# A fused pooled-attention and four-expert kernel: the first group's head is rebuilt around an early F32 load of its queries

## The chip, the cores and the metric

The kernel runs on one core of one Trainium2 chip. The metric is device time in microseconds (us) of one launch. The kernel before was run three times: 553.23, 553.50 and 553.97, median 553.5 us.

## The reference, cut to what matters

There are 8 batches with 8 heads, 576 tokens and 64 values per head. Keys and values are averaged over runs of 8 tokens, so each head has 72 pooled rows. The attention output becomes 4608 rows of 512, and four expert networks are summed over it with weights from `domain_probs`.

```python
k_p = k.reshape(B, H, 72, 8, 64).mean(axis=3)      # v_p likewise
scores = (q @ k_p.T) / 8
attn = exp(scores - max(scores))
attn = attn / (sum(attn) + 1e-9)
x = (attn @ v_p)  ->  rows of tokens, 512 columns (8 heads x 64)
p = domain_probs / (domain_probs.sum(-1) + 1e-9)
out = sum over e of p[:, e] * (relu(x @ w1[e]) @ w2[e])   # w1 512x1024, w2 1024x512
```

## The kernel before, in words

**Tiles and groups.** Tokens go in tiles of 128 (36 tiles, index `t`), four tiles to a group of 512 (9 groups). A tile of attention is: `turn_q` (four transposes on TensorE into PSUM, copy on ScalarE), `scores` (four products of 144 columns, two heads each), `less_max` (maximum and subtraction on VectorE), `expo` (ScalarE), `normalise` (sums, reciprocal and scaling on VectorE), `attn_T` (five transposes, copy), `context` (products with the values, copy into `xT`, the transposed input of the experts). From tile 8 on (`by_dma`) the transposes are DMA transposes on SP's queue, and the division is done on the context's rows instead.

**Keys and values.** A batch's 576 pooled rows lie on partitions in five blocks (the last has 64 rows, `TAIL`), with 8 x 64 values to a row. `fold` adds halves three times over on VectorE. `prep_k` multiplies the folded keys by `mask_k`, which puts each head's rows into its half of 128 columns, and `prep_kT` turns the result. `prep_v2` multiplies the folded values by `mask_v` into the block matrix `vbd`. Both masks are made on VectorE from `own`, which GpSimd makes with two selections.

**Experts.** `up` is one block of 128 hidden columns for a whole group (four products of 512 columns), `up_tile` is all 1024 hidden columns for one tile (32 products of 128 columns, L445), `down` (L462) is eight products of 512 columns for one tile, and `collect` adds the weighted result into `acc`.

**Order.** The order of every queue is the order in which the code is written; nothing is rescheduled. After the head, a loop of 36 steps (9 groups x 4 experts) with 12 slots each runs `up` of the next step and `down` of this one, and a plan puts the attention of later groups into its slots (`plan_tile`, `plan_batch`).

**The head** is all before that loop: the first batch's keys and values, group 0's four tiles, and expert 0's first tiles. Tile 0 must pass through the whole attention chain before the first `up_tile` can start. `idle_products(n)` runs `n` products of zeros (128x512) on TensorE; nothing reads their result. `split_q(c)` copies tile `c`'s rows of `qg`, the queries of group 0 as loaded, into `qrow[c]`.

**Loads.** All large loads are issued on GpSimd's queue (POOL), which casts F32 to BF16: keys of batch 0 in three pieces, `qg`, values, then weights, later keys, values and queries. A load waits for the one issued eight before it, so POOL's issues also tell when earlier loads landed. SP's queue loads `domain_probs` (`dp0`, `dpr`) at the start, and later does the DMA transposes and the output.

Of the kernel before, what the change touches and what calls it, by code (L numbers as in the profile page):

```python
# [10 lines left out]
ALU = mybir.AluOpType  # L11
AX = mybir.AxisListType
# [5 lines left out]
def kernel(  # L18
# [101 lines left out]
    def load_w2(e):  # L120
        nc.gpsimd.dma_start(
            out=w2_sb[e][:], in_=moe_w2[e].rearrange("(fb p) d -> p fb d", p=P)
        )

    dp0 = const.tile([P, TPG, E], F32, name="dp0")
    nc.sync.dma_start(
        out=dp0[:], in_=moe_domain_probs[0:G].rearrange("(p c) e -> p c e", c=TPG)
# [7 lines left out]
    still = const.tile([P, G], BF16, name="still")  # L137
    nc.vector.memset(still[:], 0.0)
    load_rows(kraw[0], k[0], ((0, 2), (2, 4)))
    qg = raw.tile([P, H, TPG, D], BF16, name="qg")  # L140
    nc.gpsimd.dma_start(
        out=qg[:], in_=q[0][:, 0:G, :].rearrange("h (p c) d -> p h c d", c=TPG)
    )

    own = const.tile([P, NPAIR, 2, 2], BF16, name="own")
    nc.gpsimd.memset(own[:], 1.0)
    for sign, base in ((1, 0), (-1, SP - 1)):
# [2 lines left out]
            base=base, channel_multiplier=sign,  # L150
            pattern=[[sign * (P - PW), NPAIR], [sign * P, 2], [-sign * SP, 2]],
        )
    ident = const.tile([P, P], BF16, name="ident")
    make_identity(nc, ident[:])
    load_v(0)
    load_w1(0)
    load_w2(0)
    load_w1(1)
    for c in range(TPG):
        qrow[c] = qpool.tile([P, H, D], BF16, name="qrow")  # L160
    ident32 = const.tile([NL, NL], F32, name="ident32")
    make_identity(nc, ident32[:])
    load_w2(1)
    load_w1(2)
    load_k(1)
    load_q(TPG)
    load_v(1)
    load_q(TPG + 1)
    load_q(TPG + 2)
    load_w2(2)  # L170
    load_w1(3)
    load_q(TPG + 3)
    load_w2(3)

    p_sb = const.tile([P, E, NT], F32, name="p_sb")
    ds0 = const.tile([P, TPG], F32, name="ds0")
    nc.vector.reduce_sum(out=ds0[:], in_=dp0[:], axis=AX.X)
    nc.vector.tensor_scalar_add(out=ds0[:], in0=ds0[:], scalar1=1e-9)
    nc.vector.reciprocal(out=ds0[:], in_=ds0[:])
    nc.vector.tensor_tensor(  # L180
        out=p_sb[:, :, 0:TPG].rearrange("p e c -> p c e"), in0=dp0[:],
        in1=ds0[:].unsqueeze(2).to_broadcast([P, TPG, E]), op=ALU.mult,
    )

    for t in (*kraw, *vraw):
        nc.vector.memset(t[TAIL:P, NB - 1, :], 0.0)
    for t in attn:
        nc.vector.memset(t[:, ROWS:NB * P], 0.0)

    mask_v = const.tile([P, NPAIR, 2, 2, D], BF16, name="mask_v")  # L190
    mask_k = const.tile([P, NB, 2, D], BF16, name="mask_k")
    nc.vector.tensor_copy(
        out=mask_v[:].rearrange("p a z y d -> p (a z y) d"),
        in_=own[:].rearrange("p a z y -> p (a z y)").unsqueeze(2).to_broadcast(
            [P, NPAIR * 4, D]
        ),
    )
    nc.vector.tensor_copy(out=mask_k[:, 0], in_=mask_v[:, 0, 0])
    nc.vector.tensor_add(
        out=mask_k[:, 1:NPAIR], in0=mask_v[:, 1:NPAIR, 0], in1=mask_v[:, 0:NPAIR - 1, 1]  # L200
    )
    nc.vector.tensor_copy(out=mask_k[:, NPAIR], in_=mask_v[:, NPAIR - 1, 1])
# [81 lines left out]
    def by_dma(t):  # L284
        return t >= 2 * TPG

    def turn_q(t):
        qT[t] = soft.tile([P, NPAIR, P], BF16, name="qT")
        if by_dma(t - 1):
            nc.sync.dma_start_transpose(  # L290
                out=qT[t][:], in_=qrow[t][:].rearrange("p h d -> p (h d)")
            )
            return
        ps = ps_t.tile([P, NPAIR, P], BF16, tag="t", name="qT_ps")
        for pair in range(NPAIR):
# [4 lines left out]
        nc.scalar.copy(out=qT[t][:], in_=ps[:])  # L300

    def scores(t):
# [7 lines left out]
                )  # L310
        scs[t] = sc

    def less_max(t):
        sc = scs.pop(t)
        view = sc[:, :, 0:2 * PW].rearrange("p g (h j) -> p g h j", j=SP)
        mx = soft.tile([P, 2, 4], F32, name="mx")
        nc.vector.reduce_max(out=mx[:], in_=view, axis=AX.X)  # L317
        d_sb = soft.tile([P, 2, 4, SP], F32, name="d_sb")
        nc.vector.tensor_tensor(  # L319
            out=d_sb[:], in0=view,  # L320
            in1=mx[:].unsqueeze(3).to_broadcast([P, 2, 4, SP]), op=ALU.subtract,
        )
        st[t] = d_sb

    def expo(t):
        if by_dma(t):
            nc.scalar.activation(  # L329
                out=attn[t % 2][:, 0:ROWS].rearrange("p (h j) -> p h j", j=SP),  # L330
                in_=st[t][:].rearrange("p g h j -> p (g h) j"),
                func=ACT.Exp, scale=EXP_SCALE,
            )
# [31 lines left out]
    def attn_T(t, copy=nc.scalar.copy):  # L365
# [6 lines left out]
            nc.tensor.transpose(ps[:, i, :], attn[t % 2][:, i * P:(i + 1) * P], ident[:])  # L372
        copy(out=attnT[t][:], in_=ps[:])  # L373

    def context_rows(t):
        ps = ps_t.tile([P, DM], F32, tag="t", name="x_ps")  # L380
        for b, _, n, at in segments(t * P, P):
            flat = vbd[b][:].rearrange("p a z y d -> p (a z y d)")
            for i in range(NB):
                c0, c1 = max(0, 4 * i - 1), min(4 * NPAIR, 4 * i + 2)
                h0 = max(0, 2 * i - 1)
# [12 lines left out]
        return x_sb  # L398
# [103 lines left out]

    def plan_tile(t, slot, turn=0):
        exp, norm, move, sum_v = (3, 4, 3, 8) if by_dma(t) else (4, 5, 8, 10)
        if t + TPG < NT and not by_dma(t):
            at(slot, load_q, t + TPG)
        at(slot + turn, turn_q, t)
        at(slot + 2, scores, t)
        at(slot + 2, less_max, t)
        at(slot + exp, expo, t)  # L510
        at(slot + move, attn_T, t)
        at(slot + norm, sums if by_dma(t) else normalise, t)
        at(slot + sum_v, context, t)
        if by_dma(t):
            at(slot + sum_v, gate, t)
            if t + TPG < NT:
                at(slot + sum_v, load_q, t + TPG)

    at(SLOTS - 4, domain_probs)
    at(SLOTS - 2, prep_k, 1)  # L520
    at(SLOTS, prep_kT, 1)
    at(SLOTS, prep_v, 1)
    at(SLOTS, load_k, 3)
    at(SLOTS, load_v, 3)
    for i, slot in enumerate((0, 4, 8, 12)):
        plan_tile(TPG + i, SLOTS + slot, -1 if i else 0)
    done_batches, waiting = 2, []
    for g in range(2, NG):
        for i in range(TPG):
            t = g * TPG + i  # L530
# [11 lines left out]


    def split_q(c):
        nc.vector.tensor_copy(out=qrow[c][:], in_=qg[:, :, c, :])  # L545
# [7 lines left out]
    prep_k(0, ((0, 2), (2, NB)))  # L553
    prep_kT(0, nc.scalar.copy)
    idle_products(4)
    split_q(0)
    turn_q(0)
    split_q(1)
    idle_products(1)
    scores(0)  # L560
    turn_q(1)
    less_max(0)
    expo(0)
    split_q(2)
    idle_products(3)
    fold(vraw[0], 0, NB, 4)
    scores(1)
    turn_q(2)
    idle_products(5)
    normalise(0)  # L570
    prep_v2(0)
    attn_T(0)
    idle_products(2)
    context(0)
    less_max(1)
    expo(1)
    up_tile(0, 0)
    scores(2)
    split_q(3)
    normalise(1)  # L580
    less_max(2)
    for t in range(1, TPG):
        if t == 1:
            turn_q(3)
        attn_T(t)
        if t + 1 < TPG:
            expo(t + 1)
        down(0, t - 1, 0, FB // 2)
        context(t)
        if t == 1:  # L590
            scores(3)
        down(0, t - 1, FB // 2, FB)
        up_tile(0, t)
        if t + 1 < TPG:
            normalise(t + 1)
        if t == 1:
# [48 lines left out]
```

## Time and profile before

| what | value |
|---|---|
| median of three runs | 553.5 us |
| profiled execution: time / span from first to last instruction | 555.25 us / 553.2 us |
| TensorE busy (matmul) | 533.0 us, 96% of the span |
| VectorE, ScalarE busy | 266.9 us, 212.0 us |
| mean granted clock of TensorE | 0.995 |
| read from memory | 45.16 MB |

The profile is of one execution. Rows of its timeline give the start, the duration, the engine (PE is TensorE's products, PEld its weight loads, DVE is VectorE, ACT is ScalarE, POOL is GpSimd, SPq is SP's queue), the line of the kernel, the operation, and what ended the idle time before it. A row with `x4` is a merged group of four instructions. The table of stages gives busy time of each engine in a stretch of time, the granted clock (1.00 is full), and what the DMA queues moved.

### The profile page before, as it was taken

The numbers are of one execution on the slowest core, as the hardware profiler recorded it, in microseconds if no ns is written. First come the engines' busy times: TensorE is split into PE (matmuls) and PEld (weight loads), VectorE is DVE, ScalarE is ACT, GpSimd is POOL, SyncE is SP. The second block draws the span as 40 slices with busy tenths as digits, with TensorE's granted clock in tenths as the row PEclk, the third lists the DMA queues.
The fourth block names the chain that finished last, engine by engine and source line by source line (L and its number), as shares of the span: only waits on it lengthen the run. The fifth ranks groups of instructions, "written<-read, shape, count | busy, mean of one in ns | idle before, by whom it ended". The sixth has DMA issues, their size and how long they took to land.

```text
span 553.2 us, 7201 instructions
## 1 busy us (share of the span) xinstructions
PE 533.0 (96%) x2837; PEld 260.0 (47%) x2892; DVE 266.9 (48%) x458; ACT 212.0 (38%) x352; POOL 71.9 (13%) x121
## 2 busy tenths in 40 slices
PE   2799999999999999999999999999999999999996
PEld 1574554444444444444444444444444444444443
DVE  4875657444744445544564444744474444422222
ACT  1455653333333333333333333333333333333330
POOL 7224311210111100121011100110010000000000
PEclk9899999999999999999999999999999999999999
DMA  9999995455345544366535553334333321111002
GB/s 137 207 206 197 203 123 109 68 80 80 75 86 79 79 78 80 53 84 87 113 44 78 78 116 41 52 42 97 61 53 41 87 52 32 21 39 38 1 0 76
DMA packets 110688, 45.30 MB, mean 82 GB/s; under 512 B 87584, under 2 KB 106016, under 8 KB 110656
## 3 DMA queue, kind: packets, MB, share of 16 engines
q0 software_dynamic: 52512, 22.55, 33.1%
q1 hardware_dynamic: 58144, 22.30, 16.8%
q8 instruction: 22, 0.36, 0.3%
q14 instruction: 10, 0.08, 0.0%
HBM read 45.16 MB, written 9.44 MB: 99 GB/s over the span
## 4 chain that ended last, share of the span: by engine, by line
PE 94%; DMA 2%; DVE 1%; issue 1%; ACT 1%; POOL 0%; ACTq 0%; POOLq 0%
PE o_ps L462 44%; PE h_ps L429 43%; PE x_ps L386 2%; PE sc L306 2%; PE h_ps L445 2%; DMA qg<-in_q_dram 2%; PE x_ps L412 1%; PE qT_ps L296 0%; ACT attnT L373 0%; POOL kraw L79 0%; ACT qT L300 0%; DVE vraw L225 0%; PE at_ps L372 0%; DVE qrow L545 0%; DVE vbd L270 0%
## 5 line engine op out<-in xcount | busy, mean ns | idle before, releaser
L433 ACT ACTIVATE h_sb<-h_ps 128x512 bf16<-128x512 f32 x280 | 167.2, 597 | 296.4 <-PE h_ps L429 289.8
L429 PE MATMUL h_ps<-xT,w 128*128 128x512 bf16 x1088 | 271.8, 379 | 1.5
L462 PE MATMUL o_ps<-w,h_sb 128*128 128x512 bf16 x1129 | 269.9, 379 | 1.4
L462 PEld LDWEIGHTS <-h_sb 128*128 128x128 bf16 x1152 | 112.3, 98 | 133.6
L477 DVE SCALAR_TENSOR_TENSOR acc<-o_ps,p_sb,acc 128x512 f32<-128x512 f32 x108 | 81.0, 750 | 180.1 <-PE o_ps L462 177.4
L429 PEld LDWEIGHTS <-w 128*128 128x128 bf16 x1120 | 105.9, 98 | 116.9
L473 DVE TENSOR_SCALAR acc<-o_ps,p_sb 128x512 f32<-128x512 f32 x36 | 27.0, 750 | 59.7 <-PE o_ps L462 59.7
L501 POOL COPY gated<-x_sb 1x1 bf16<-1x1 bf16 x28 | 7.8, 280 | 362.5 <-DVE x_sb L392 362.5
L317 DVE TENSOR_REDUCE mx<-sc 128x8 f32<-128x576 f32 x36 | 27.2, 756 | 13.4 <-PE sc L306 13.4
L107 POOL DMA_DIRECT2D qrow<-in_q_dram x36 | 30.5, 848 | 20.0 <-DMA w<-in_moe_w_dram 9.9
L319 DVE TENSOR_TENSOR d_sb<-sc,mx 128x576 f32<-128x576 f32 x36 | 27.3, 758 | 1.2
L392 DVE SCALAR_TENSOR_TENSOR x_sb<-x_ps,rs 128x512 bf16<-128x512 f32 x28 | 19.4, 692 | 12.1 <-PE x_ps L386 11.7
L350 DVE TENSOR_REDUCE es<-attn 128x8 f32<-128x576 bf16 x28 | 20.8, 743 | 0.0
L329 ACT ACTIVATE attn<-d_sb 128x576 bf16<-128x576 f32 x28 | 19.1, 682 | 3.2
L306 PE MATMUL sc<-kT,qT 128*128 128x144 bf16 (+1 forms) x160 | 15.5, 231 | 0.4 <-ACT qT L300 0.3
L306 PEld LDWEIGHTS <-qT 128*128 128x128 bf16 (+1 forms) x160 | 11.4, 102 | 9.6 <-ACT qT L300 1.7
L386 PEld LDWEIGHTS <-attnT 128*128 128x128 bf16 (+1 forms) x155 | 11.7, 100 | 7.2 <-issue 1.3
L386 PE MATMUL x_ps<-vbd,attnT 128*128 128x192 bf16 (+5 forms) x155 | 14.2, 231 | 0.0
L225 DVE TENSOR_TENSOR kraw<-kraw 128x1280 bf16<-128x1280 bf16 (+5 forms) x18 | 10.6, 589 | 2.3 <-DMA kraw<-in_k_dram 2.0
L225 DVE TENSOR_TENSOR vraw<-vraw 128x1280 bf16<-128x1280 bf16 (+1 forms) x16 | 10.5, 653 | 0.2
L255 PE MATMUL kT_ps<-ident,kpad 128*128 128x128 bf16 x10 | 1.2, 264 | 9.4 <-DVE kpad L240 9.4
L445 PE MATMUL h_ps<-xT,w 128*128 128x128 bf16 x128 | 9.3, 239 | 0.7 <-ACT xT L418 0.7
(61 smaller groups left out, 152.7 us busy)
## 6 DMA issues: line engine op xcount, KB each, us to landing
out_dram<-acc SPq DMA_DIRECT2D x36, 256.0 KB, 2.0
vraw<-in_v_dram POOLq DMA_DIRECT2D x8, 512.0 KB, 8.2
w<-in_moe_w_dram POOLq DMA_DIRECT2D x8, 512.0 KB, 15.7
w<-in_moe_w_dram POOLq DMA_DIRECT2D x4, 1024.0 KB, 16.9
kraw<-in_k_dram POOLq DMA_DIRECT2D x7, 512.0 KB, 7.2
qrow<-in_q_dram POOLq DMA_DIRECT2D x28, 128.0 KB, 3.9
kraw<-in_k_dram POOLq DMA_DIRECT2D x2, 256.0 KB, 4.7
kraw<-in_k_dram POOLq DMA_DIRECT2D x8, 64.0 KB, 6.8
```

The lines of the kernel that those rows point to most:

```text
L107: nc.gpsimd.dma_start(out=qrow[t][at:at + n], in_=q[b][:, tok:tok + n, :].rearrange("h p d -> p h d"),)
L225: nc.vector.tensor_add(out=rows[:, i0:i1, 0:w], in0=rows[:, i0:i1, 0:w], in1=rows[:, i0:i1, w:2 * w],)
L306: nc.tensor.matmul(sc[at:at + n, pair // 2, (pair % 2) * PW:(pair % 2 + 1) * PW], lhsT=qT[t][:, pair, at:at + n], rhs=kT[b][:].rearrange(" ...
L317: nc.vector.reduce_max(out=mx[:], in_=view, axis=AX.X)
L319: nc.vector.tensor_tensor(out=d_sb[:], in0=view, in1=mx[:].unsqueeze(3).to_broadcast([P, 2, 4, SP]), op=ALU.subtract,)
L350: nc.vector.reduce_sum(out=es[:], in_=e, axis=AX.X)
L386: nc.tensor.matmul(ps[at:at + n, h0 * D:(h0 + c1 - c0) * D], lhsT=attnT[t][:, i, at:at + n], rhs=flat[:, c0 * D:c1 * D], start=(i == 0), s ...
L429: nc.tensor.matmul(ps[:], lhsT=w1_sb[e][:, kc, fb * P:(fb + 1) * P], rhs=xT[g][:, kc, :], start=(kc == 0), stop=(kc == KC - 1),)
L433: nc.scalar.activation(out=hs[s][:, fb, :], in_=ps[:], func=ACT.Relu)
L462: nc.tensor.matmul(ps[:], lhsT=hs[s][:, fb, i * P:(i + 1) * P], rhs=w2_sb[e][:, fb, :], start=(fb == 0), stop=(fb == FB - 1),)
L473: nc.vector.tensor_scalar_mul(out=accs[t][:], in0=ps[:], scalar1=p_sb[:, e, t:t + 1])
L477: nc.vector.scalar_tensor_tensor(out=accs[t][:], in0=ps[:], scalar=p_sb[:, e, t:t + 1], in1=accs[t][:], op0=ALU.mult, op1=ALU.add,)
```

## The change

The head is written anew; the loop of steps stays, but for the slots of a few loads.

- **Queries.** `qg` becomes F32 and is loaded by SP as the first transfer of its queue; `split_q` moves from VectorE to ScalarE. Turned queries get a pool of four buffers.
- **Keys of batch 0.** They are folded in the three pieces in which they land, the last fold writes both halves of `kpad0` by a broadcast, without a mask. After the turn, two copies on VectorE take each head's rows out of PSUM into a zeroed `kT[0]`.
- **Tile 0.** The exponentials go undivided into `attn[0]`. Their sums come from TensorE (`sums0`, products with `own`), and the division is done on the context's rows (`context_rows`), which are then turned by four transposes (`turn_x0`).
- **Values of batch 0.** Eight accumulating products with the identity sum them in PSUM (`sum_values0`), and two VectorE instructions spread them with the mask (`spread_values0`).
- **Order.** More idle products stand between the steps; the masks and `dp0`'s normalisation come later; `down` of tile 0 comes after `up_tile` of tile 1; `prep_v(1)` is planned four slots later; POOL issues values before the identity and `own`, and the second batch's keys and expert 2's first weights ahead of expert 1's second weights. Later query loads are issued three tiles ahead, and batch 3's keys and values come later.

```diff
+    qg = raw.tile([P, H, TPG, D], F32, name="qg")
+    nc.sync.dma_start(
+        out=qg[:], in_=q[0][:, 0:G, :].rearrange("h (p c) d -> p h c d", c=TPG)
+    )
     dp0 = const.tile([P, TPG, E], F32, name="dp0")
...
     load_rows(kraw[0], k[0], ((0, 2), (2, 4)))
-    qg = raw.tile([P, H, TPG, D], BF16, name="qg")
-    nc.gpsimd.dma_start(
-        out=qg[:], in_=q[0][:, 0:G, :].rearrange("h (p c) d -> p h c d", c=TPG)
-    )
+    load_v(0)
+    ident = const.tile([P, P], BF16, name="ident")
+    make_identity(nc, ident[:])
...
     load_w1(0)
     load_w2(0)
     load_w1(1)
...
+    load_k(1)
...
+    load_w1(2)
+    load_q(TPG)
     load_w2(1)
-    load_w1(2)
-    load_k(1)
-    load_q(TPG)
+    load_q(TPG + 1)
     load_v(1)
...
+    def in_rows(t):
+        return t == 0 or by_dma(t)
+
     def turn_q(t):
-        qT[t] = soft.tile([P, NPAIR, P], BF16, name="qT")
+        qT[t] = qtp.tile([P, NPAIR, P], BF16, name="qT")
...
     def expo(t):
-        if by_dma(t):
+        if in_rows(t):
...
-        if t + TPG < NT and not by_dma(t):
-            at(slot, load_q, t + TPG)
...
-            if t + TPG < NT:
-                at(slot + sum_v, load_q, t + TPG)
+            if t + 3 < NT:
+                at(slot + sum_v, load_q, t + 3)
...
-    at(SLOTS, prep_v, 1)
-    at(SLOTS, load_k, 3)
-    at(SLOTS, load_v, 3)
+    at(SLOTS + 4, prep_v, 1)
...
-    done_batches, waiting = 2, []
+    done_batches, waiting = 2, [(load_k, 3), (load_v, 3)]
...
     def split_q(c):
-        nc.vector.tensor_copy(out=qrow[c][:], in_=qg[:, :, c, :])
+        nc.scalar.copy(out=qrow[c][:], in_=qg[:, :, c, :])
...
+    def fold_keys0(p1, i0, i1):
+        rows = kraw[0][0:p1, i0:i1]
+        for n in (4, 2):
+            w = n * D
+            nc.vector.tensor_add(
+                out=rows[:, :, 0:w], in0=rows[:, :, 0:w], in1=rows[:, :, w:2 * w]
+            )
+        twice = [p1, i1 - i0, 2, D]
+        nc.vector.tensor_tensor(
+            out=kpad0[0:p1, i0:i1], in0=rows[:, :, 0:D].unsqueeze(2).to_broadcast(twice),
+            in1=rows[:, :, D:2 * D].unsqueeze(2).to_broadcast(twice), op=ALU.add,
+        )
...
+    def sum_values0():
+        ps = ps_h.tile([P, NB, D], F32, tag="h", name="v_ps")
+        for r in range(POOL):
+            nc.tensor.matmul(
+                ps[:], lhsT=ident[:], rhs=vraw[0][:, :, r * D:(r + 1) * D],
+                start=(r == 0), stop=(r == POOL - 1),
+            )
+        return ps
...
+    idle_products(14)
+    split_q(0)
+    split_q(1)
+    turn_q(0)
+    turn_q(1)
+    for part in ((P, 0, 2), (P, 2, 4), (TAIL, 4, 5)):
+        fold_keys0(*part)
+        turn_keys0(*part)
+        idle_products(2)
+    take_keys0()
+    make_mask_v()
+    scores(0)
+    split_q(2)
+    turn_q(2)
+    less_max(0)
+    split_q(3)
+    expo(0)
+    idle_products(2)
+    spread_values0(sum_values0())
+    attn_T(0)
+    scores(1)
+    maxima(1)
+    idle_products(2)
+    sums0()
+    turn_q(3)
+    idle_products(1)
+    xT[0] = grp.tile([P, KC, G], BF16, name="xT")
+    x0 = context_rows(0)
     idle_products(4)
...
+    turn_x0(x0)
+    less(1)
+    expo(1)
     idle_products(2)
...
     up_tile(0, 0)
     scores(2)
-    split_q(3)
     normalise(1)
+    idle_products(4)
     less_max(2)
+    domain_probs0()
     for t in range(1, TPG):
-        if t == 1:
-            turn_q(3)
         attn_T(t)
         if t + 1 < TPG:
             expo(t + 1)
-        down(0, t - 1, 0, FB // 2)
+        if t == 1:
+            idle_products(3)
+        else:
+            down(0, t - 1, 0, FB // 2)
         context(t)
         if t == 1:
             scores(3)
-        down(0, t - 1, FB // 2, FB)
-        up_tile(0, t)
+            up_tile(0, t)
+            down(0, t - 1)
+        else:
+            down(0, t - 1, FB // 2, FB)
+            up_tile(0, t)
...
+        if t == TPG - 1:
+            make_mask_k()
         collect(0, t - 1)
+    load_q(2 * TPG)
     load_k(2)
+    load_q(2 * TPG + 1)
     load_v(2)
+    load_q(2 * TPG + 2)
```

More of the change, by code (lines that the diff above doesn't have):

```diff
@@ L57 @@
     qpool = ctx.enter_context(tc.tile_pool(name="qpool", bufs=8))
+    qtp = ctx.enter_context(tc.tile_pool(name="qtp", bufs=TPG))
     soft = ctx.enter_context(tc.tile_pool(name="soft", bufs=2))
@@ L152 @@
         )
-    ident = const.tile([P, P], BF16, name="ident")
-    make_identity(nc, ident[:])
-    load_v(0)
     load_w1(0)
@@ L160 @@
         qrow[c] = qpool.tile([P, H, D], BF16, name="qrow")
+    load_k(1)
     ident32 = const.tile([NL, NL], F32, name="ident32")
     make_identity(nc, ident32[:])
+    load_w1(2)
+    load_q(TPG)
     load_w2(1)
-    load_w1(2)
-    load_k(1)
-    load_q(TPG)
+    load_q(TPG + 1)
     load_v(1)
-    load_q(TPG + 1)
     load_q(TPG + 2)
-    load_w2(2)
     load_w1(3)
     load_q(TPG + 3)
+    load_w2(2)
     load_w2(3)
[L175 to L186, printed above, removed]
+    nc.vector.memset(vraw[0][TAIL:P, NB - 1, :], 0.0)
     for t in attn:
@@ L191, with make_mask_v, make_mask_k, domain_probs0 @@
     mask_k = const.tile([P, NB, 2, D], BF16, name="mask_k")
[L192 to L202, printed above, removed]
+    def make_mask_v():
+        nc.vector.tensor_copy(
+            out=mask_v[:].rearrange("p a z y d -> p (a z y) d"),
+            in_=own[:].rearrange("p a z y -> p (a z y)").unsqueeze(2).to_broadcast(
+                [P, NPAIR * 4, D]
+            ),
+        )
+    def make_mask_k():
+        for t in (*kraw, vraw[1]):
+            nc.vector.memset(t[TAIL:P, NB - 1, :], 0.0)
+        nc.vector.tensor_copy(out=mask_k[:, 0], in_=mask_v[:, 0, 0])
+        nc.vector.tensor_add(
+            out=mask_k[:, 1:NPAIR], in0=mask_v[:, 1:NPAIR, 0], in1=mask_v[:, 0:NPAIR - 1, 1]
+        )
+        nc.vector.tensor_copy(out=mask_k[:, NPAIR], in_=mask_v[:, NPAIR - 1, 1])
+    p_sb = const.tile([P, E, NT], F32, name="p_sb")
+    def domain_probs0():
+        ds0 = const.tile([P, TPG], F32, name="ds0")
+        nc.vector.reduce_sum(out=ds0[:], in_=dp0[:], axis=AX.X)
+        nc.vector.tensor_scalar_add(out=ds0[:], in0=ds0[:], scalar1=1e-9)
+        nc.vector.reciprocal(out=ds0[:], in_=ds0[:])
+        nc.vector.tensor_tensor(
+            out=p_sb[:, :, 0:TPG].rearrange("p e c -> p c e"), in0=dp0[:],
+            in1=ds0[:].unsqueeze(2).to_broadcast([P, TPG, E]), op=ALU.mult,
+        )
     def domain_probs():
@@ L311, in scores, with by_head, maxima, less @@
         scs[t] = sc
-    def less_max(t):
[L314 to L323, printed above, removed]
+    mxs = {}
+    def by_head(t):
+        return scs[t][:, :, 0:2 * PW].rearrange("p g (h j) -> p g h j", j=SP)
+    def maxima(t):
+        mxs[t] = soft.tile([P, 2, 4], F32, name="mx")
+        nc.vector.reduce_max(out=mxs[t][:], in_=by_head(t), axis=AX.X)
+    def less(t):
+        st[t] = soft.tile([P, 2, 4, SP], F32, name="d_sb")
+        nc.vector.tensor_tensor(
+            out=st[t][:], in0=by_head(t),
+            in1=mxs[t][:].unsqueeze(3).to_broadcast([P, 2, 4, SP]), op=ALU.subtract,
+        )
+    def less_max(t):
+        maxima(t)
+        less(t)
     def expo(t):
-        if by_dma(t):
+        if in_rows(t):
             nc.scalar.activation(
@@ L373, in attn_T, with chunk @@
         copy(out=attnT[t][:], in_=ps[:])
+    def chunk(i):
+        return max(0, 4 * i - 1), min(4 * NPAIR, 4 * i + 2), max(0, 2 * i - 1)
     def context_rows(t):
@@ L383, in context_rows @@
             for i in range(NB):
-                c0, c1 = max(0, 4 * i - 1), min(4 * NPAIR, 4 * i + 2)
-                h0 = max(0, 2 * i - 1)
+                c0, c1, h0 = chunk(i)
                 nc.tensor.matmul(
@@ L551, in idle_products @@
             nc.tensor.matmul(ps[:], lhsT=still[:, 0:P], rhs=still[:], start=True, stop=True)
-    prep_k(0, ((0, 2), (2, NB)))
-    prep_kT(0, nc.scalar.copy)
-    idle_products(4)
[L556 to L572, printed above, removed]
+    kT[0] = prep.tile([P, NB, P], BF16, name="kT")
@@ new lines @@
+    nc.vector.memset(kT[0][:], 0.0)
+    kpad0 = prep.tile([P, NB, 2, D], BF16, name="kpad")
+    kT_ps = ps_h.tile([P, NB, P], BF16, tag="h", name="kT_ps")
+    def fold_keys0(p1, i0, i1):
+        rows = kraw[0][0:p1, i0:i1]
+        for n in (4, 2):
+            w = n * D
+            nc.vector.tensor_add(
+                out=rows[:, :, 0:w], in0=rows[:, :, 0:w], in1=rows[:, :, w:2 * w]
+            )
+        twice = [p1, i1 - i0, 2, D]
+        nc.vector.tensor_tensor(
+            out=kpad0[0:p1, i0:i1], in0=rows[:, :, 0:D].unsqueeze(2).to_broadcast(twice),
+            in1=rows[:, :, D:2 * D].unsqueeze(2).to_broadcast(twice), op=ALU.add,
+        )
@@ new lines, in turn_keys0, with take_keys0 @@
+    def turn_keys0(p1, i0, i1):
+        for i in range(i0, i1):
+            nc.tensor.transpose(
+                kT_ps[:, i, 0:p1], kpad0[0:p1, i].rearrange("p z d -> p (z d)"),
+                ident[0:p1, 0:p1],
+            )
+    def take_keys0():
+        for z in range(2):
+            dst, src = (
+                x[z * D:(z + 1) * D].rearrange("x i p -> x (i p)")[:, 0:ROWS].rearrange(
+                    "x (a y j) -> x a y j", y=2, j=SP
+                )[:, :, z]
+                for x in (kT[0], kT_ps)
+            )
+            nc.vector.tensor_copy(out=dst, in_=src)
@@ new lines, in sum_values0, with spread_values0 @@
+    def sum_values0():
[4 more added lines that the diff above has]
+                start=(r == 0), stop=(r == POOL - 1),
+            )
+        return ps
+    def spread_values0(ps):
+        vbd[0] = prep.tile([P, NPAIR, 2, 2, D], BF16, name="vbd")
+        for z in range(2):
+            nc.vector.tensor_tensor(
+                out=vbd[0][:, :, z],
+                in0=ps[:, z:z + NPAIR].unsqueeze(2).to_broadcast([P, NPAIR, 2, D]),
+                in1=mask_v[:, :, z], op=ALU.mult,
+            )
@@ new lines, in sums0 @@
+    def sums0():
+        ps = ps_o.tile([P, H], F32, tag="o_ps", name="es_ps")
+        flat = own[:].rearrange("p a z y -> p (a z y)")
+        for i in range(NB):
+            c0, c1, h0 = chunk(i)
+            nc.tensor.matmul(
+                ps[:, h0:h0 + c1 - c0], lhsT=attnT[0][:, i], rhs=flat[:, c0:c1],
+                start=(i == 0), stop=(i == NB - 1), skip_group_check=True,
+            )
+        es = soft.tile([P, H], F32, name="es")
+        nc.vector.tensor_scalar_add(out=es[:], in0=ps[:], scalar1=1e-9)
+        rss[0] = soft.tile([P, H], F32, name="rs")
+        nc.vector.reciprocal(out=rss[0][:], in_=es[:])
@@ new lines, in turn_x0 @@
+    def turn_x0(x_sb):
+        ps = ps_t.tile([P, KC, P], BF16, tag="t", name="xT_ps")
+        for kc in range(KC):
+            nc.tensor.transpose(ps[:, kc], x_sb[:, kc * P:(kc + 1) * P], ident[:])
+        nc.scalar.copy(out=xT[0][:, :, 0:P], in_=ps[:])
+    idle_products(14)
[9 more added lines that the diff above has]
+    make_mask_v()
@@ L573 @@
+    scores(0)
[15 more added lines that the diff above has]
+    x0 = context_rows(0)
+    idle_products(4)
+    turn_x0(x0)
+    less(1)
+    expo(1)
     idle_products(2)
-    context(0)
-    less_max(1)
-    expo(1)
     up_tile(0, 0)
     scores(2)
-    split_q(3)
```

## The prediction, made before the change was run

> **What bounds the kernel now.** The page comes first: the span, the slices, the chain that ended last.
>
> ```profile
> span 553.2 us, 7201 instructions
> PE   2799999999999999999999999999999999999996
> PE 94%; DMA 2%; DVE 1%; issue 1%; ACT 1%; POOL 0%; ACTq 0%; POOLq 0%
> ```
>
> TensorE is the chain, and only the first two slices (28 us) have room. The table of stages says how full it is later and how full early:
>
> ```profile
> 18.00:20.00 2.00, 0.84 (x7) 0.39 (x7) 1.86 (x6) 0.35 (x1) 0.14 (x2) 1.00 1.25 207
> 20.00:22.00 2.00, 0.87 (x10) 0.59 (x10) 1.97 (x4) 0.92 (x2) 0.50 (x1) 1.00 1.25 209
> 22.00:24.00 2.00, 2.00 (x22) 2.00 (x22) 1.38 (x5) 0.98 (x2) 0.00 (x0) 0.54 1.24 206
> 100.00:200.00 100.00, 99.47 (x506) 47.29 (x514) 47.27 (x79) 37.05 (x62) 13.62 (x23) 1.00 0.51 76
> ```
>
> Columns: stage, its length, busy PE, weight loads, DVE, ACT, POOL, granted clock, DMA share, GB/s. From 100 us on PE is full, so the change is worth what it moves the start of full work, and nothing else. At 18 to 22 us DVE is full (1.86, 1.97) and PE is not (1.71 of 4 us); just after, the clock is half. The timeline gives the fixed points:
>
> ```profile
> 3.37 0.93 POOL L141 DMA_DIRECT2D qg<-in_q_dram  x1
> 11.74 0.50 DVE L545 COPY qrow<-qg 128x512 bf16<-128x512 bf16 x2 [2.42 <-DMA qg<-in_q_dram]
> 13.37 0.66 PE L306 MATMUL sc<-kT,qT 128*128 128x144 bf16 x4 [0.25 <-ACT qT L300]
> 19.15 0.28 PEld L372 LDWEIGHTS <-attn 128*128 128x128 bf16 x5 [1.96 <-DVE attn L358]
> 21.95 3.42 PE L445 MATMUL h_ps<-xT,w 128*128 128x128 bf16 x32 [0.68 <-ACT xT L418]
> 30.67 0.44 PE L372 MATMUL at_ps<-ident,attn 128*128 128x128 bf16 x5
> 39.72 5.34 PE L429 MATMUL h_ps<-xT,w 128*128 128x512 bf16 x23
> ```
>
> Queries land at 11.7 and release the first scores at 13.37; tile 0's softmax and values on DVE hold the first expert product until 21.95. From the turn of tile 2's weights (30.67) both kernels have the same work on PE, so I follow one number: when that turn starts. (Keys are folded by 9.3, before the queries are there.)
>
> **The queries' landing** is the largest unknown. Today they are third in POOL's queue. In the change SP issues them first, where dp0 now stands (issued 0.82, landed 2.6). The bytes double, 1.05 MB as F32, and POOL's queue carries keys, then values, at once. Rows for the rates:
>
> ```profile
> 3.00:4.00 1.00, 0.00 (x0) 0.00 (x0) 0.87 (x4) 0.00 (x0) 1.00 (x2) 1.00 0.87 102
> 5.00:6.00 1.00, 0.00 (x0) 0.00 (x0) 0.85 (x3) 0.00 (x0) 0.93 (x4) 1.00 1.25 195
> 13.00:14.00 1.00, 0.75 (x7) 0.63 (x7) 0.00 (x0) 0.32 (x1) 0.00 (x0) 1.00 1.25 206
> 549.00:549.50 0.50, 0.05 (x1) 0.00 (x0) 0.41 (x1) 0.00 (x0) 0.00 (x0) 1.00 1.00 377
> ```
>
> A casting load writes 206 GB/s, so reads 412 GB/s of F32; an F32 store on SP's queue moves 377 GB/s. Alone, the queries land at 0.82 + 1.8 + 1.05/0.377 = 5.4: the lower end. Served after keys and values they land where values land now, 14.5 (a wait on POOL ends there at 14.55): the upper end. Between: SP's bytes run from about 1.9, the keys' from 3.0, so some 0.4 MB goes ahead; 0.65 MB at half of 412 takes 3.2, at a third (a key request reads 2 KB, a query request 1 KB) 4.7. Bytes end at 6.2 or 7.7, and landing follows by 0.7 (keys now) to 1.7 (queries now). I take 8.2, nearest the half share. The keys' last piece slips from 7.4 to about 8.4 and is folded by 9.4, under the queries.
>
> The Trainium skill, "DMA: Bandwidth & Descriptors", section "Queues, rings and completion order", speaks against the change: an engine takes its queues in turn by whole packets, not by bytes. By its packet of up to 4096 B ("SWDGE vs HWDGE vs iDMA"), an estimate: four key requests for one query request would leave the queries 46 GB/s and land them near 18, some 8 us slower in all; four for four is the third share above.
>
> **Landing to first scores.** Three queues now stand still for data: ACT's at the first split (all qT copies and the exponential behind it), PE's at turn_q(0) (key transposes and scores behind it), and later PE's at the value sums (tile 0's turn and scores(1) behind). ACT splits (0.37, DVE's mean for that copy, to 0.69, ACT's 640 columns; I take ACT's 0.59 for 512): two before anything is turned, 9.4. PE then has turn_q(1), five key transposes and four idle products in its queue before the keys are complete: 9 small products and 4 long ones. The row of five idle products took 1.24, that of four at the start 1.91: 1.4 us at full clock, 2.8 at half. Fourteen idle products fill 1.3 to some 6.5, then PE is empty until 8.9. Today 1.71 busy in 4 us was followed by half clock; I take the middle, 2.1. Then two copies of the keys on DVE, 0.36 each by its 0.49 for 640 columns, and 0.2 of hand-overs: scores(0) at 12.45, 0.9 earlier than now.
>
> The skill's "TensorE: Matmul & The Clock Gate", Part 1, lets the clock fall after an idle window of about 3.4 us; by it alone a 2.4 us gap keeps full clock, and the first scores would be 0.7 earlier than my middle.
>
> **First scores to first expert product.** Removed from the path: sums and normalise (0.74, 0.48, 0.20, 0.76), folds (0.81, 0.48, 0.33) and vbd (0.76 for two) on DVE. In place, one chain: scores 0.41, mask_v still running 0.28, maximum 0.76, subtraction 0.76, exponential 0.69, five transposes 0.45, copy 0.69, sums0 with turn_q(3) and an idle product 0.70, context 0.50, x_sb 0.69, four transposes 0.40, copy 0.59: 6.92 and eleven hand-overs of 0.05, 7.45 in all. Now it is 8.58. Expert product at 19.9.
> Cover: the value sums (eight products of 320 columns, 1.26 with the drain) and two spreads from PSUM (0.69 each, as x_sb) take 2.7 after the values; with values no earlier than today's 14.5 that is 17.2, and context is due at 17.5. If values come later, every us counts in full. The first w1 (19.9 now) has the same bytes ahead and is there.
>
> **The clock.** The first 32 products took 3.42 at half clock, 1.95 in the third tile. In the new chain PE is busy some 6.5 of 7.45 us, against 1.71 of 4 now: I count full clock, -1.47. Without it the term is nil.
>
> **From there to the turn of tile 2.** Now 25.37 to 30.67, 5.3. In the change scores 0.25, four idle products 0.88, transposes 0.45, copy 0.69 (three idle products beneath), exponential 0.69, xT copy 0.59, hand-overs 0.15, up_tile 1.80, the whole of down 1.73: 7.2. The change pays 1.9 here, since down now comes after the second expert tile.
> Sum: 19.9 + 1.95 + 7.2 = 29.05 against 30.67: -1.6; with the splits, which may be shorter, I say -1.7.
>
> **At nothing.** mask_k and memsets (1.8) fall where DVE is empty (0.00 busy from 36 to 38), else a late collect holds an o_ps buffer. w2(1) stands behind 1.8 MB more, 8.6 us (at 206 GB/s) after the POOL wait that it ends at 35.2 now: 43.8, needed near 49 by down of expert 1 (51.05 now). POOL makes the identity before own, not after, and the values' issue comes before both; neither is waited for by 8.9. k3 and v3 come 30 and 42 slots later and still lead their folds by 37 or more; load_q leads by 19 slots of 1.2 us against landings of 3.4; vbd(1) at slot 16 is used at 22. domain_probs0 (0.72) stands before tile 2's sums with PE busy. If one cover fails it costs its own length, under 2.
>
> **Rivals.**
> Slower: SP's queue is served behind POOL's. For it:
>
> ```profile
> L249 SPq DMA_TRANSPOSE kT<-kpad x6: 1267/1267/1278, 92.5 to 410.4; - x6
> DMA to landing us min/median/max: 3.9/4.0/4.2
> ```
>
> These are issued beside a query load; the attention transposes of the same size land in 2.6. Each us of landing past 8.2 moves the first scores by one, so the gain is gone at 9.9 and 1.1 is lost at 11.0; 11.7 gives +1.8, 14.5 +4.6. Price +3: 556.5. Against it: SP issues first and nothing else moves until 3.
> Faster: queries land by 7.0, PE stays at full clock, and the keys set the pace: last piece 8.3, fold 1.0, transposes and copies 1.1, first scores 10.4, two earlier than above: 549.7.
> No change: queries near 9.5, or the first expert product at half clock again: 553.3.
>
> **How the numbers follow.** The profiled execution took 555.25 for a span of 553.2; less 1.7 it is 553.55; the runs' median stands 1.75 under it, so 551.8. Chances: forecast 0.36 (550.4 to 552.7, the clock's two ends), faster rival 0.25, no change 0.15, slower 0.24. 0.2% is 1.1 us, about what a measurement can tell. Faster by more: 0.25 and most of the forecast, 0.56; within: 0.18; slower: 0.26. The range goes from the faster rival, 549.2, into the slower one, 556.0.
>
> **What would show it.** Right: qg released near 8.2, first scores near 12.4, first up product near 19.9 and 1.95 long, the tile 2 turn near 29. Wrong if ACT's first copy waits past 10 for qg, if clock events fall inside the first expert product, or if the step loop's first product moves by other than the turn.

## The result

The changed kernel takes 556.12 us (median of ten runs, 554.65 to 556.4); the kernel before, run beside it on the same chip, 553.68 (ten runs, 553.23 to 555.0). The ratio is 1.0034, 95% interval 1.0023 to 1.0045: slower by 2.4 us by the medians, where the forecast was 1.7 faster. The profiled run took 556.4.

The page of the changed kernel: span, TensorE's busy share in 40 slices, the chain by engine, GB/s per slice.

```profile
span 554.4 us, 7323 instructions
PE   7899998999999999999999999999999999999997
PE 93%; DMA 3%; DVE 2%; ACT 1%; issue 0%; POOL 0%; SPq 0%; POOLq 0%
GB/s 200 206 200 200 199 8 137 74 80 79 122 82 83 84 59 99 53 84 74 116 48 77 84 116 41 52 41 98 60 54 40 74 74 32 21 39 38 1 0 77
```

The first slice is fuller than before (7 against 2), but that says little of the head's gain: the fourteen opening products of zeros alone take 4.97 of its 13.9 us. New is an 8 in the seventh slice (83 to 97 us); in the slice ahead of it the DMA queues moved 8 GB/s.

The timeline has the fixed points of the head: when queries and keys land, the first scores, the first turn of weights, the first expert product, the turn of tile 2.

```profile
0.81 0.45 SPq L130 DMA_DIRECT2D qg<-in_q_dram  x1
6.54 1.14 ACT L565 CAST qrow<-qg 128x512 bf16<-128x512 f32 x2 [4.45 <-DMA qg<-in_q_dram]
7.79 0.75 DVE L584 TENSOR_TENSOR kraw<-kraw 128x512 bf16<-128x512 bf16 x2 [5.68 <-DMA kraw<-in_k_dram]
11.82 0.41 PE L320 MATMUL sc<-kT,qT 128*128 128x144 bf16 x4 [0.18 <-DVE kT L608]
14.84 0.45 PE L394 MATMUL at_ps<-ident,attn 128*128 128x128 bf16 x5 [0.87 <-ACT attn L351]
19.01 1.95 PE L469 MATMUL h_ps<-xT,w 128*128 128x128 bf16 x32 [0.24 <-ACT xT L648]
27.92 0.44 PE L394 MATMUL at_ps<-ident,attn 128*128 128x128 bf16 x5
```

The turn of tile 2 starts 2.75 earlier than before (30.67). Placing the weighted results in `acc` (VectorE, one per tile and expert) side by side, the lead is 2.5 to 3.4, mostly 2.9, up to the sixteenth; from the seventeenth to the last the changed kernel is 1.64 late, without drift. One event costs 4.5 us. The timeline of that place:

```profile
88.42 0.70 POOL L525 COPY gated<-x_sb 1x1 bf16<-1x1 bf16 x1 [29.07 <-DVE x_sb L416]
89.07 0.88 POOL L108 DMA_DIRECT2D qrow<-in_q_dram  x1
89.62 1.28 SPq L259 DMA_TRANSPOSE kT<-kpad  x1
89.94 0.76 POOL L80 DMA_DIRECT2D kraw<-in_k_dram  x1
90.69 0.56 POOL L84 DMA_DIRECT2D kraw<-in_k_dram  x1
97.41 0.64 PE L320 MATMUL sc<-kT,qT 128*128 128x144 bf16 x4 [2.88 <-DMA kT<-kpad]
```

POOL stands behind the first `gate` for 29 us. (`gate` copies one element of a tile's context rows, so that the loads written behind it are issued only when that tile is done.) When it opens, POOL issues a query load and then, at once, batch 3's keys (0.59 MB as BF16). Between the two, SP issues the transpose that turns batch 2's keys into `kT`. The scores of the first tile that uses it wait 2.88 us for it, and TensorE has nothing else in its queue that may run. The chain of waits gives the transpose 7.65 us; the view of the tile `kT` has a landing of 7.7 among six, where before none was over 4.2:

```profile
L259 SPq DMA_TRANSPOSE kT<-kpad x6: 1267/1274/2282, 89.6 to 412.0; - x6
DMA to landing us min/median/max: 3.7/4.2/7.7
```

The wait is not all. The table of stages (the columns as in the prediction) shows the clock after it:

```profile
94.00:97.00 3.00, 0.53 (x3) 0.03 (x1) 0.46 (x1) 0.60 (x1) 0.00 (x0) 1.00 1.01 182
97.00:98.00 1.00, 0.59 (x5) 0.61 (x6) 0.00 (x0) 0.00 (x0) 0.00 (x0) 0.53 1.18 270
98.00:99.00 1.00, 1.00 (x4) 0.29 (x2) 0.88 (x2) 0.00 (x0) 0.00 (x0) 0.50 0.64 195
99.00:100.00 1.00, 1.00 (x4) 0.32 (x3) 0.63 (x1) 0.21 (x1) 0.00 (x0) 0.50 0.04 16
100.00:101.00 1.00, 1.00 (x5) 0.46 (x4) 0.00 (x0) 0.96 (x2) 0.00 (x0) 0.77 0.00 0
```

TensorE is empty for 2.9 us and then runs at half clock for 3.4 (0.94, 1, 1 and 0.46 of the four stages). Half of the 3 busy us in that time is lost: 2.9 + 1.5 = 4.4, the event's 4.5. The ten runs show the two parts too: the three at a mean clock of 1.000 took 554.65 to 554.9, still 2.9 above the version without the wait (551.73, below); the seven at 0.997 took, with one exception, 556.1 to 556.4.

### The profile page after: what moved, and what is told of

Same layout as the page of the kernel before. It is cut to its first block, busy times and chain, and to the rows that moved or that the text cites. A ratio compares the mean times of both kernels' runs of the same rounds, so it can differ in the third digit from the quotient of the medians.

```text
span 554.4 us, 7323 instructions
## 1 busy us (share of the span) xinstructions
PE 542.0 (98%) x2929; PEld 261.3 (47%) x2929; DVE 264.7 (48%) x456; ACT 213.5 (39%) x355; POOL 70.6 (13%) x120
## 4 chain that ended last, share of the span: by engine, by line
PE 93%; DMA 3%; DVE 2%; ACT 1%; issue 0%; POOL 0%; SPq 0%; POOLq 0%
PE o_ps L486 44%; PE h_ps L453 43%; PE x_ps L410 2%; PE sc L320 2%; DMA kT<-kpad 1%; PE h_ps L469 1%; DMA kraw<-in_k_dram 1%; PE x_ps L436 1%; PE o_ps L571 0%; DVE acc L501 0%; PE at_ps L394 0%; ACT attnT L395 0%; PE qT_ps L310 0%; DVE kraw L235 0%; DVE vraw L235 0%
## 5 line engine op out<-in xcount | busy, mean ns | idle before, releaser
L453 PE MATMUL h_ps<-xT,w 128*128 128x512 bf16 x1120 | 275.2, 380 | 0.0
L571 PE MATMUL o_ps<-still 128*128 128x512 bf16 x38 | 11.8, 436 | 1.3 <-DVE still L144 1.3
L235 DVE TENSOR_TENSOR vraw<-vraw 128x1280 bf16<-128x1280 bf16 (+1 forms) x14 | 9.2, 654 | 0.2
L235 DVE TENSOR_TENSOR kraw<-kraw 128x1280 bf16<-128x1280 bf16 (+1 forms) x14 | 9.0, 640 | 0.2
L469 PE MATMUL h_ps<-xT,w 128*128 128x128 bf16 x128 | 7.8, 219 | 0.7 <-ACT xT L442 0.4
## 6 DMA issues: line engine op xcount, KB each, us to landing
w<-in_moe_w_dram POOLq DMA_DIRECT2D x4, 1024.0 KB, 16.2
```

The costliest lines, as they stand in the source:

```text
L453: nc.tensor.matmul(ps[:], lhsT=w1_sb[e][:, kc, fb * P:(fb + 1) * P], rhs=xT[g][:, kc, :], start=(kc == 0), stop=(kc == KC - 1),)
```

## The experiments

First theory: the new plan of loads, not the head, loses the time. Rivals: the head is worth less than its sum, or the plan loses by something other than the keys. The first four runs:

**The head without the new plan.** In the changed kernel the loads go back to the places of before:

```diff
+        if t + TPG < NT and not by_dma(t):
+            at(slot, load_q, t + TPG)
...
-            if t + 3 < NT:
-                at(slot + sum_v, load_q, t + 3)
+            if t + TPG < NT:
+                at(slot + sum_v, load_q, t + TPG)
...
+    at(SLOTS, load_k, 3)
+    at(SLOTS + 4, load_v, 3)
...
-    done_batches, waiting = 2, [(load_k, 3), (load_v, 3)]
+    done_batches, waiting = 2, []
...
-    load_q(2 * TPG)
     load_k(2)
-    load_q(2 * TPG + 1)
     load_v(2)
-    load_q(2 * TPG + 2)
```

> The changed kernel with the loads planned as before the change: later queries four tiles ahead, batch 3's keys at slot 12 and values at slot 16 (behind the moved fold of batch 1's values), no query loads at the end of the head. Theory A (the loss is the wait at 97.4 us for batch 2's turned keys, which batch 3's key load beside them delays): the wait of 2.9 us and the half clock after it are gone, kT's longest landing is near 4.2, time 551.5 to 552.4. Theory B (the head arrives 2.9 us early and meets the output stores of group 0 there, whatever the plan of loads): kT still lands after 7 us or so, time 555 to 556.5. Theory C (half of the head's 2.9 us was the half-clock stretch of one profiled run of the kernel before, and most runs of it do not have that): with the wait gone only 1.3 to 1.5 remains, time near 552.3.

Measured: 551.86 (551.79 to 552.52, five runs), ratio 0.9969 [0.9957, 0.9981]. `kT` lands in 4.4 at most, nothing waits for it, and the lead of 2.8 holds to the end.

**The new plan without the head.** The same lines the other way, in the kernel before.

> The kernel before, with only the change's plan of loads (queries three tiles ahead, batch 3's keys and values behind tiles 8 and 9). Theory A: the keys' turn lands after 7 us and TensorE waits some 2.9 us and loses up to 1.7 to the half clock: 556.5 to 558.3. Theory B: no wait without the early head, time 553.5 to 554.5.

Measured: 556.72 (555.52 to 558.57, six runs), ratio 1.0057 [1.0039, 1.0075]. `kT` takes up to 7.0 and the scores wait 2.2. So the plan costs 3.0 on the old head and 4.3 on the new (556.12 against 551.86), and the head alone gains 1.9.

**Later keys, by seven slots.**

```diff
-                at(base + 6, load, b)
+                at(base + (13 if t == 2 * TPG else 6), load, b)
```

> The changed kernel, with batch 3's keys alone issued 7 slots later (slot 49, after tile 9's scores). Theory A, if the 590 KB of keys do the delaying: kT lands in about 4.2, no wait, 551.5 to 552.4. If tile 11's query load does it, or the stores: kT still after 7, 555 to 556.5.

Measured: 555.29 (553.9 to 556.56, ten runs), ratio 1.0024 [1.0014, 1.0035]; landing 6.9, wait 2.1. As a test of the keys it failed: a slot sets only the order in POOL's queue. POOL was standing behind the gate, and as no other load stood in between the keys were issued at 89.72, right behind the query load as in the changed kernel.

**A later query load.**

```diff
-                at(slot + sum_v, load_q, t + 3)
+                at(slot + sum_v + (7 if t == 2 * TPG else 0), load_q, t + 3)
```

> The changed kernel, with tile 11's query load alone issued 7 slots later (slot 49); batch 3's keys stay at slot 42 and so come 0.9 us sooner after the gate. If the keys do the delaying: kT lands as late as in the change or later, 555 to 557. If the query load does: 551.5 to 552.4.

Measured: 558.0 (557.17 to 558.41, four runs), ratio 1.0074 [1.006, 1.0089]: worse. The same queue, with the query load behind the keys, has the keys ahead of the transpose:

```profile
89.73 0.76 POOL L80 DMA_DIRECT2D kraw<-in_k_dram  x1
90.27 1.28 SPq L259 DMA_TRANSPOSE kT<-kpad  x1
90.48 0.55 POOL L84 DMA_DIRECT2D kraw<-in_k_dram  x1
91.01 0.92 POOL L108 DMA_DIRECT2D qrow<-in_q_dram  x1
98.85 0.50 PE L320 MATMUL sc<-kT,qT 128*128 128x144 bf16 x4 [3.66 <-DMA kT<-kpad]
```

The landing goes to 8.4, the wait to 3.66. That points at the keys; that their place half a microsecond ahead of the transpose makes it worse rests on this one trace, beside 6.9 to 7.7 in the three with the keys 0.3 behind it.

**Keys behind the next gate.** To move a load in time, another wait must come before it:

```diff
-            if waiting:
+            if waiting and t > 2 * TPG:
                 load, b = waiting.pop(0)
```

> The changed kernel, but loads that wait for a slot are handed out from tile 9's slot on, so batch 3's keys stand in POOL's order behind the gate of tile 9 (and their values behind that of tile 10) instead of behind the gate of tile 8. Theory: batch 2's turned keys land late because 1.2 MB of batch 3's keys are issued beside their transpose. Then it lands in 3.9 to 4.6 us again, the scores of the first step-loop tile that uses it wait for nothing, and the time is 551.5 to 552.6. Rival: the new plan costs by itself, by query loads three tiles ahead or POOL standing still behind the first gate, whatever load follows it. Then the landing stays above 6 us and the time at 555 or more.

Measured: 551.73 (551.71 to 552.07, six runs), ratio 0.9968 [0.9957, 0.998]. Its timeline:

```profile
88.25 0.70 POOL L525 COPY gated<-x_sb 1x1 bf16<-1x1 bf16 x1 [28.91 <-DVE x_sb L416]
88.90 0.88 POOL L108 DMA_DIRECT2D qrow<-in_q_dram  x1
89.46 1.28 SPq L259 DMA_TRANSPOSE kT<-kpad  x1
94.20 0.41 PE L320 MATMUL sc<-kT,qT 128*128 128x144 bf16 x4
104.09 0.76 POOL L80 DMA_DIRECT2D kraw<-in_k_dram  x1
```

`kT` lands in 4.4 at most, and the scores have no wait. The query load is still issued beside the transpose, POOL still stands 29 us behind the gate, and the sixth slice is still nearly without DMA traffic (16 GB/s), which therefore costs nothing by itself; batch 3's keys come 14 us later, and the loads that wait in line behind them one tile later. One line is worth 4.4 us by the medians. The rival (the plan itself costs) falls. Why a load beside it delays the transpose so much, no run shows.

The other runs take the head apart, or trim it. They start from one of the two versions without the loss: the next two and the one without opening products from that with the old plan (551.86), the rest from that with the keys behind the next gate (551.73). The kernel before had a median of 553.63 to 553.73 beside all of them.

**Queries on POOL's queue again** (BF16, third, behind the keys' pieces), the rest of the new head kept:

> The new head with the old plan of loads (551.86 us), but the queries of group 0 are loaded as BF16 by POOL's queue behind the keys, as in the kernel before; all else of the new head stays. Theory that SP's queue is what the head lives on: queries land near 11.7 as before, first scores go from 11.8 to some 14.5 to 16, since the splits and turns then lie behind the landing and the values' sums stand next in TensorE's order, and the time is 553.5 to 556, all of the head's gain gone. Rival, that the shorter chain behind the scores carries the gain: first scores near 13.4 as before and the time 552.3 to 553.

Measured: 556.34 (556.04 to 557.15, four runs), ratio 1.0055 [1.004, 1.0071]. Queries are there at 10.97, first scores at 15.83 (before: 13.37), first expert product at 23.04. TensorE stands still from 6.88 and runs at half clock from 9.6 to 16.4. The new order of queues behind a late landing is slower than the old head.

**Queries third on SP's queue**, behind the two small loads, so issued 0.93 us later:

> The new head with the old plan of loads, but SP issues the queries as third transfer, behind the two small loads of domain_probs, so about 1.3 us later (near 2.1), when the keys' loads have been issued for about 1 us. If SP's queue is served ahead of POOL's by its kind, the queries land 5.7 after issue as now, near 7.8, and the keys' bytes wait for them. If it was only ahead because it was first, the two share: queries land near 9 or later, or the keys' first piece comes first, and is folded before 7.8.

Measured: 556.3 in its one run. Its timeline:

```profile
1.31 1.55 POOL L80 DMA_DIRECT2D kraw<-in_k_dram  x2 [0.80 <-POOLq L746]
1.74 0.41 SPq L139 DMA_DIRECT2D qg<-in_q_dram  x1
7.09 0.75 DVE L588 TENSOR_TENSOR kraw<-kraw 128x512 bf16<-128x512 bf16 x2 [4.98 <-DMA kraw<-in_k_dram]
11.28 1.14 ACT L569 CAST qrow<-qg 128x512 bf16<-128x512 f32 x2 [9.18 <-DMA qg<-in_q_dram]
```

Issued 0.4 us after the keys' first piece instead of 0.5 before it, the same transfer takes 9.5 to land instead of 5.7 (5.2 to 5.7 in the nine profiled runs with the whole load first). So it was not served first for being on SP's queue, but, in these runs, for being issued first.

**Queries in two halves**, tiles 0 and 1 first, tiles 2 and 3 as SP's fourth transfer:

```diff
+    load_q0(0)          # qgs[0]: rows c = 0, 1 of each run of four
     dp0 = ...           # dp0 and dpr as before
+    load_q0(1)          # qgs[1]: rows c = 2, 3
...
-        nc.scalar.copy(out=qrow[c][:], in_=qg[:, :, c, :])
+        nc.scalar.copy(out=qrow[c][:], in_=qgs[c // 2][:, :, c % 2, :])
```

> The changed kernel with the late gate, but the queries of group 0 come in two transfers, tiles 0 and 1 first in SP's queue and tiles 2 and 3 behind the two small loads, some 1.3 us after the first. Theory: the queries' bytes go first and the keys pay for it (0.52 MB at 372 to 389 GB/s is 1.4 us), so with half of them behind the keys' first piece the keys are folded 0.8 to 1.4 earlier and first scores come near 10.5 instead of 11.7; the values then set more of the rest, and the first expert product moves by 0.5 to 1.2: time 550.5 to 551.2. Rival, that the second half is served ahead of the keys as well, or the values' landing sets the chain: 551.5 to 551.9.

Measured: 553.84 (552.79 to 555.34, twelve runs), ratio 1.0001 [0.9991, 1.0012]; a miss. The first half is there at 4.99 and the keys' first piece at 6.50, as the theory has it, but the second half then shares the queues with the keys:

```profile
6.50 0.75 DVE L588 TENSOR_TENSOR kraw<-kraw 128x512 bf16<-128x512 bf16 x2 [4.39 <-DMA kraw<-in_k_dram]
9.26 0.75 DVE L588 TENSOR_TENSOR kraw<-kraw 128x512 bf16<-128x512 bf16 x2 [1.68 <-DMA kraw<-in_k_dram]
12.68 0.62 ACT L569 CAST qrow<-qg 128x512 bf16<-128x512 f32 x1 [4.58 <-DMA qg<-in_q_dram]
```

The keys' second piece is no earlier (8.91 unsplit), so first scores come at 12.00, tile 2's split at 12.68 holds TensorE's queue ahead of the values' sums, and the clock is half from 12.8 to 16.2.

**Values folded on VectorE** instead of summed by products (`prep_v(0)` in place of `spread_values0(sum_values0())`):

> The changed kernel with the late gate for batch 3's keys (551.73 us), but batch 0's values are folded and spread on VectorE at the place where the changed head spreads them, instead of summed by eight products. Theory that the parts of the new chain add up as predicted: three folds (0.81, 0.48, 0.33) and two spreads (0.76 together) replace 1.29 of spreads behind the sums, so vbd is ready some 1.1 later, near 16.2, the maximum of tile 1 and the division's two small steps stand behind it, and x_sb starts 0.2 to 0.9 later than 17.03: time 551.9 to 552.7. Rival, that it is hidden beside exponential, turn and copy: within 0.2 of 551.73.

Measured: 553.38 (552.5 to 554.24, ten runs), ratio 0.9991 [0.9982, 1.0001]. The length alone is as the theory says: the three runs at a clock of 0.999 to 1.000 took 552.5 to 552.6, 0.8 more. The others lose 0.7 to 1.7 more, and in the profiled one, one of them, the clock is half from 15.7 to 19.1. The eight products had filled TensorE from 12.6 to 13.8, where it now stands still:

```profile
12.00:13.00 1.00, 0.73 (x8) 0.24 (x5) 0.97 (x2) 0.66 (x2) 0.64 (x2) 1.00 1.23 205
13.00:14.00 1.00, 0.00 (x0) 0.00 (x0) 0.97 (x3) 0.49 (x2) 0.90 (x3) 1.00 1.25 208
14.00:15.00 1.00, 0.31 (x6) 0.31 (x7) 0.97 (x2) 0.64 (x1) 0.09 (x1) 1.00 1.23 203
15.00:16.00 1.00, 0.85 (x10) 0.41 (x9) 0.93 (x4) 0.69 (x1) 0.69 (x1) 0.85 1.26 210
16.00:17.00 1.00, 1.00 (x11) 0.72 (x12) 1.00 (x3) 0.29 (x1) 0.05 (x1) 0.50 1.24 205
```

**Division before the turn**, with `normalise(0)` behind the exponential and `context(0)` straight into `xT`:

> The changed kernel with the late gate, but tile 0 is divided before its turn, as in the kernel before: sums, reciprocal and scaling on VectorE behind the exponential, then the turn, and the context goes straight to xT without rows and a second turn. Theory: 1.9 of normalise on the path replaces 0.7 of x_sb, 0.4 of turn and 0.1 to 0.3 of sums0, and the spreads of the values (1.3) come behind it on VectorE instead of beside the exponential; the first expert product goes from 18.84 to 19.5 to 20.4, the time to 552.3 to 553.3. Rival: the two are even and the time is within 0.3 of 551.73.

Measured: 554.45 (552.77 to 555.98, ten runs), ratio 1.0007 [0.9994, 1.002]. Three runs took 552.8 to 552.9, inside the expectation; the others lose 1.5 to 3.2 more. In the profiled run, one of the others, TensorE does nothing from 14 to 17 us and then runs at half clock until 20.7, and the first expert product starts at 21.81. That the half clock is the whole of this loss is not shown: 552.82, one of the quick three, has the same mean clock (0.997).

**No opening products of zeros** (`idle_products(14)` left out):

> The new head with the old plan of loads, without the fourteen opening products of zeros. Theory: they hold TensorE's clock at full speed for the short products of the head, and without them the granted clock is half until 3 to 4 us after the key turns begin; first scores 0.3 to 0.8 later, the time up by 0.3 to 1.2. Rival: the clock rises with the products between the key turns in time for the first expert product, and the time is within 0.3 of 551.86.

Measured: 552.51 (552.46 to 553.01, ten runs), ratio 0.9981 [0.9972, 0.999]: 0.65 for fourteen products. Until about 13 the products have the lengths of half clock (the first scores take 0.69 instead of 0.41), though the granted clock in the table of stages reads 1.00 there; first scores come at 12.25 instead of 11.93.

**A trimmed head**, on the version with keys behind the next gate: `mask_v` ahead of the key folds, one key copy on ScalarE, splits 2 and 3 earlier, two idle products fewer:

```diff
-            nc.vector.tensor_copy(out=dst, in_=src)
+            (nc.scalar.copy if z else nc.vector.tensor_copy)(out=dst, in_=src)
...
+    split_q(2)
+    split_q(3)
+    make_mask_v()
     for part in ((P, 0, 2), (P, 2, 4), (TAIL, 4, 5)):
...
-    make_mask_v()
     scores(0)
-    split_q(2)
...
-    idle_products(4)      # ahead of less_max(2)
+    idle_products(2)
```

> The changed kernel with the late gate (551.73 us), its chain up to the first expert product trimmed where its trace shows waits: mask_v (0.69) is made ahead of the key folds, where VectorE stands still until 7.6, instead of between the key copies and the maximum; the second of the two copies of the turned keys goes to ScalarE beside the first (0.31 each); splits 2 and 3 go ahead of it; and two idle products instead of four stand before tile 1's turn. Theory: first scores at 11.4 instead of 11.7, the maximum at 11.9 instead of 12.4, then the values' landing (12.3) and their sums are next; first expert product 18.2 to 18.5 instead of 18.84, 0.3 less before tile 1's turn, time 550.8 to 551.3. Rival: the values or the clock take it back, and the time is 551.5 or more.

Measured: 551.52 (551.44 to 551.77, five runs), ratio 0.9961 [0.9947, 0.9974]. It beats both kernels and is the best of the study, but it is only 0.2 under the version that it starts from, which the two intervals don't tell apart: the rival holds. The two key copies did not run side by side: ScalarE's started at 11.41, when VectorE's was done, so first scores stayed at 11.86. Only the two idle products showed (tile 1's turn at 21.40 instead of 21.74).

## Why the prediction was wrong

**The step that failed** is in "At nothing": "k3 and v3 come 30 and 42 slots later and still lead their folds by 37 or more". The lead is true, and it prices only when the keys are needed. What a 0.59 MB load delays at its new place was not asked, nor where POOL would be: standing behind the gate, so that the query load and the keys come out one behind the other, the keys 0.3 us behind a transpose that TensorE needs within 5 us. Its price was 4.4 us (556.12 against 551.73), more than the whole head. "If one cover fails it costs its own length, under 2" was too small as well: the wait alone was 2.9, and 3.4 us at half clock follow it.

The row that warned was on the table. The `kT` transposes, 3.9 to 4.2 beside a query load against 2.6 for those of attention, were read as evidence on the queries' queue and as the slower rival's support. Read for the transposes, they suggest that a load beside one delays it; a query load is 0.13 MB, batch 3's keys are over four times that.

**The slower rival** ended on the right side by a mechanism that did not occur. Queries waited for nothing of POOL's (6.54), so its 24% was chance on the wrong cause. The range held no time above 556.0; the result is 0.1 outside.

**The queries' landing**: 6.54, forecast 8.2, bounds 5.4 and 14.5. Sharing at a half or a third was wrong: from 4 to 5 us the queues move 389 GB/s, near the 377 of the F32 store and far from the 206 of casting loads, and the first fold of the keys starts later than before (7.79 against 6.32). So the queries' bytes go ahead, and the keys come after.

```profile
3.00:4.00 1.00, 1.00 (x4) 0.40 (x3) 0.00 (x0) 0.00 (x0) 1.00 (x2) 1.00 0.88 274
4.00:5.00 1.00, 1.00 (x5) 0.31 (x3) 0.00 (x0) 0.00 (x0) 0.94 (x3) 1.00 1.09 389
5.00:6.00 1.00, 1.00 (x6) 0.39 (x4) 0.00 (x0) 0.00 (x0) 0.84 (x5) 1.00 1.18 290
```

The Trainium skill, "DMA: Bandwidth & Descriptors", section "Queues, rings and completion order", has each engine alternate between its queues by packets; the estimate from it, queries near 18, is far off for a transfer that is first. With the order reversed by 0.9 us the two do share (9.5 to land), and which rule they follow then is open.

**Landing to first scores**: 5.28 against 4.25 forecast. The keys, not the queries, became the later input: first fold at 7.79, last fold done at 10.85 (forecast 9.4). This is the faster rival's mechanism, but the second piece is folded from 9.08, where it had the last at 8.3, and the folds, three parts one after the other on VectorE, take 2.8 us in all (0.75, 0.29, 0.75, 0.29, 0.53, 0.22) instead of 1.0 behind the last piece. Both errors together: first scores at 11.82, 0.6 better than forecast.

**First scores to first expert product**: 7.19, forecast 7.45; right, term by term. The runs show that its parts are worth their length (values by products 0.8, late division 1.1, by the quickest runs without them); the medians without them stand higher still (553.38 and 554.45), and the profiled runs show a stretch at half clock.

**The clock**: 1.95 for the first 32 products, as said. But the term of -1.47 belonged to the one profiled run of before. In the run with only the new plan, the old head kept full clock:

```profile
21.32 1.95 PE L445 MATMUL h_ps<-xT,w 128*128 128x128 bf16 x32 [0.67 <-ACT xT L418]
28.86 0.44 PE L372 MATMUL at_ps<-ident,attn 128*128 128x128 bf16 x5
```

There tile 2's turn is at 28.86 instead of 30.67, and against that run the new head gains only 28.86 - 27.92 = 0.94. Of 29 runs of before in one comparison 23 had a clock of 0.999 or more, so the half clock that the sum removes is not in the median. The sum takes it off twice: as 1.47, and again within the 1.75 by which the runs' median stands under the profiled run; with the old plan of loads that distance is 0.2 (552.05 against 551.86). Those 23 took 552.9 to 554.1, while the new head without the loss took 551.7 to 552.1; what spreads the old head by 1.2 us at full clock was not looked into.

The skill's "TensorE: Matmul & The Clock Gate", Part 1, asks for an idle window of about 3.4 us before the clock falls; here it fell at 97.06, after 2.5 us without a product, and stayed down for 3.4, the page's window. Waits of 2.1 and 2.2 did not bring it down in two profiled runs, but with the queries third it fell 2.2 after the last opening product (8.6 against 6.4): the length of the wait alone does not decide.

**From there to the turn of tile 2**: 6.96, forecast 7.2. Sum at that turn -2.75, forecast -1.6 to -1.7. The time of the head with the old plan, 551.86, is the forecast's 551.8 to a tenth, but by errors that cancel: by the profile the head was over 1 us better than its sum, and 1.47 of that sum was not there to be won in the median. The forecast's range, "550.4 to 552.7, the clock's two ends", doesn't follow from the sum either: 1.4 and 2.8 in place of its 2.1 give 551.1 to 552.5.

## What to carry to other kernels

A load that is issued later is not free because its user is still far off: look at what stands on the DMA queues at the new place, and first of all for a small transfer that TensorE waits for. A slot behind a waiting instruction is an order, not a time, and everything queued there comes out at once when the wait ends. And where one profiled run has a stretch at half clock, see whether the other runs have it before it goes into the sum.

## What was not expected of the hardware

- The order of issue within a microsecond decides who is served: the same 1.05 MB on SP's queue lands 5.2 to 5.7 us after issue when it is issued 0.5 before POOL's first load, and 9.5 when issued 0.4 after it (one run). The batch 2 transpose lands 6.9 to 7.7 after issue with the keys 0.3 behind it, 8.4 with them 0.5 ahead (one run), and in at most 4.6 without.
- TensorE's clock is part of a short stage's price: fourteen products that nothing reads are worth 0.65 us at the start, and where the value sums or the undivided exponentials were taken away, TensorE stood still for 2.0 and 3.1 us, and a stretch of 3.4 us at half clock followed in the profiled runs.
